# Lightning attention into a Mish layer: half of the second group's first layer by two sets of seven products, and buffers and sums placed anew

## The chip, the core and the metric

The kernel runs on one core of one Trainium2 chip. The metric is the device time of one execution, in microseconds (us), lower is better. The core has five engines with a queue of instructions each, which run in order and wait for each other on semaphores: TensorE (PE in the profile, its weight loads PEld), VectorE (DVE), ScalarE (ACT), GpSimd (POOL) and SyncE (SP).

## What is computed

The reference has two parts. The first is a decayed linear attention over 4 batches, 8 heads, 768 positions and head size 64, in blocks of positions with a running state:

```
intra = (q k^T * Dmask) v
inter = (q * lam_pow) kv_state
out   = intra + inter
kv_state = lam^block * kv_state + (k * rev_pow)^T v
```

The result, as 3072 tokens of 512 features, goes through two dense layers:

```
h = x @ w_in                      # 512 -> 2048
g = h * tanh(softplus(h))         # Mish
return g @ w_out                  # 2048 -> 512
```

Inputs and result are float32; the kernel computes products in float16 with float32 sums.

## The kernel before

**Groups and blocks.** The 768 positions are cut into six groups of 128 positions (n = 0 to 5); a group has four blocks, one for each batch (b = 0 to 3), and 512 tokens. The program is one order of steps written out by hand, in which attention of a later group is strewn between the dense products of an earlier one, so that TensorE always has a product to do while the other engines prepare the next operands.

**Attention of one block.** `turn_pe` (L222) transposes k and q on TensorE (L230) and copies the result out of PSUM, by ScalarE (L238) or VectorE (L236); `turn_dma` (L240) has the DMA engines do it for two blocks. `scores` (L251) makes the products of q and k in two PSUM banks, `be` and `bo`, and VectorE multiplies them by the mask (two `sb` tiles, L262). `outputs` (L279) sums state part (L283) and masked part (L288) in bank `bz`, and VectorE scales that into `xn` (L291). `state` (L336) multiplies the decayed k (`kd`, made by `decay_k`, L249) by v into bank `bH` (L332); VectorE adds the old state (`raw`, L344) and GpSimd multiplies by the decay (`w`, L346). `xn` is then transposed into `xt`, the first layer's input, by a DMA (L296) or on TensorE (L302, copied out at L307).

**First layer.** Two forms are in use. `two_units` (L381) makes two of the 16 slices of 128 features for half of the group's tokens (256) in eight products of 128x256, in one of the banks `bA`, `bB`, `bC` in turn, and ScalarE applies Mish (L391). The other form is a set of seven products (`set_of`, `set_step`, L425 and L452): a quarter of the features, for all 512 tokens, is seen as a 2x2 by 2x2 block product and made in seven block products of four matmuls each (L445) in place of eight, after the scheme of Strassen in Winograd's form. A set needs sums of weights (`wsum`, four per set by `w_sum`, L408), sums of the input (`xsum`, four per group by `x_sums`, L423), two copies by ScalarE (`seed` L459, `p5` L467), and two additions by VectorE: L470, which adds the copy to bank `o.b` and puts it in bank `o.c` before step m7 may write `o.b` again, and L474, which makes `c22` from `o.b` before step m4 may write it. The steps come in the order m1, seed, m2, m5, m6, m7, m3, m4. Before the change group 1 (the second) is made by `two_units` alone; groups 2 to 5 by sets.

**Second layer.** Group 0 goes plainly (`dense2_plain`, L604): per block four parts of four products of 128x512 in one bank, called as `plain2`. Later groups use seven products there as well (`dense2`, L566), from sums of the weights (`tsum`, `weight_sum`, L504) and of the Mish results (`gsum`, `token_sum`, L523, called as `sums`). The last group's second layer, `dense2_alone` (L618), closes the kernel: its last products are added in three pieces (L657) into output tiles of tag `osum`, of which there are three buffers, and stored by SP's queue (L531).

**Order around the change.** After group 1's attention the program runs the 16 calls of `two_units` for group 1 (each half of the tokens by itself), with attention of group 2's first two blocks, the weight sums of set 3 (`w_sum(3, ...)`) and of set 1, and the sums of w_out between them (L758 to L817); then `plain2` for group 0 with the attention of group 2's blocks 2 and 3 (L825 to L844); then the loop over n (L860).

Of the kernel before, what the change touches and what calls it, by code (L numbers as in the profile page):

```python
# [7 lines left out]
F32 = mybir.dt.float32  # L8
# [12 lines left out]
def kernel(  # L21
# [10 lines left out]
    nc = tc.nc  # L32
    B, H, S, D = q.shape
    C = 128
# [212 lines left out]
    def decay_k(n, b, eng):  # L247
        kd[n, b] = work.tile([128, H, D], F16, name="kd", tag="kd", bufs=4)
        eng.tensor_tensor(out=kd[n, b], in0=kn[n, b], in1=bc(lk, 2, D), op=ALU.mult)  # L249
# [131 lines left out]
    def two_units(n, ni, r):  # L381

        t = bank(next_bank(), [2, HC])
        cs = slice(r * HC, r * HC + HC)
        for u in range(2):
            for kc in range(NKC):
                m = (ni + u) % 4 * 128
                nc.tensor.matmul(  # L388
                    t[:, u, :], win[ni // 4][:, kc, m : m + 128], xt[n][:, kc, cs],
                    start=(u == 0 and kc == 0), stop=(kc == NKC - 1), skip_group_check=True)  # L390
        nc.scalar.activation(h_tile(n)[:, ni : ni + 2, cs], t, AF.Mish)  # L391
# [171 lines left out]
    def osum():  # L563
        return work.tile([128, 2, HN], F32, name="osum", tag="osum", bufs=3)
# [53 lines left out]
    def dense2_alone(n):  # L618

        x, z = bank("G", [2, HN]), bank("H", [2, HN])  # L620
        y = [(bank("A", [HN]), 0, 0, HN), (bank("B", [HN // 2]), 1, 0, HN // 2),
             (bank("C", [HN // 2]), 1, HN // 2, HN)]
        keep = lambda name: work.tile([128, 2, HN], F32, name=name, tag=name, bufs=1)

        def both(p, t, fresh):
            for blk in range(2):
                product(n, p, t[:, blk, :], blk, fresh and blk == 0)

        both(1, x, True)
# [12 lines left out]
        nc.gpsimd.tensor_tensor(out=u2, in0=u3, in1=p7, op=ALU.subtract)  # L642
        for t, blk, lo, hi in y:
            product(n, 5, t, blk, True, lo, hi)
        o = osum()
        for t, blk, lo, hi in y:
            nc.vector.tensor_tensor(out=o[:, blk, lo:hi], in0=t, in1=u3[:, blk, lo:hi], op=ALU.add)
        store(n, 1, 1, o)
        both(4, z, False)
        o = osum()  # L650
        nc.vector.tensor_tensor(out=o, in0=z, in1=p1, op=ALU.add)
        store(n, 1, 0, o)
        for t, blk, lo, hi in y:
            product(n, 3, t, blk, False, lo, hi)
        for t, blk, lo, hi in y:
            o = osum()
            nc.vector.tensor_tensor(out=o[:, blk, lo:hi], in0=t, in1=u2[:, blk, lo:hi], op=ALU.add)  # L657
            store(n, 0, 1, o[:, blk : blk + 1, lo:hi], blk, lo, hi)

# [110 lines left out]
    two_units(1, 6, 0)  # L770
    later[2]()
    out1(3, "G", "e", "o")
    two_units(1, 8, 0)
    later[3]()
    two_units(1, 10, 0)
    turn_pe(2, 0, ("H", "z"))
    decay_k(2, 0, nc.vector)
    decay_k(2, 1, nc.vector)
    w_sum(1, 0, nc.vector)
    w_sum(1, 1, nc.vector)  # L780
    two_units(1, 12, 0)
    turn_dma(2, 1)

    def attend(n, b):
        scores(n, b)

    def attended(n, b, turn=None):
        then = outputs(n, b, turn)
        state(n, b, "H", nc.gpsimd)
        return then  # L790

    two_units(1, 14, 0)
    attend(2, 0)
    two_units(1, 0, 1)
    w_sum(1, 2, nc.vector)
    w_sum(1, 3, nc.vector)
    turn_pe(2, 1, ("H", "G"))
    two_units(1, 2, 1)
    attended(2, 0)
    attend(2, 1)  # L800
    two_units(1, 4, 1)
    weight_sum(0, 0)
    two_units(1, 6, 1)
    weight_sum(0, 1)
    two_units(1, 8, 1)
    attended(2, 1)
    for t, bp in (("k", 0), ("q", 0), ("v", 0)):
        load_pair(t, 3, bp)
    for i in range(2):
        weight_sum(1, i)  # L810
    two_units(1, 10, 1)
    two_units(1, 12, 1)
    two_units(1, 14, 1)
    for i in range(4):
        w_sum(3, i, nc.vector)
    weight_sum(2, 0)
    weight_sum(2, 1)  # L817

    def plain2(b, *parts):
        for part in parts:
            dense2_plain(0, b, part, "GABC"[b])

    plain2(0, 0, 1, 2, 3)  # L825
    attend(2, 2)
    decay_k(2, 2, nc.vector)
    plain2(1, 0, 1)
    attended(2, 2)
    turn_dma(3, 0)  # L830
    attend(2, 3)
    decay_k(2, 3, nc.vector)
    plain2(1, 2, 3)
    plain2(2, 0)
    last_x = attended(2, 3, "e")
    for t, bp in (("k", 1), ("q", 1), ("v", 1)):
# [23 lines left out]
    for n in range(1, NG - 1):  # L860
# [110 lines left out]
            h(1)  # L971
        mm(0, "m5", "m6")
        if not fresh:
            sums(n, 1, 0, 1)
            h(1)
        o_(0)
        fetch(("k", 0), ("q", 0))
        if fresh:
            h(1)
# [11 lines left out]
        settle()  # L991
        mm(1, "m2")
        h(1)
        mm(1, "m5", "m6")
        sums(n, 1, 2)
        h(1)
        o_(1)
        fetch(("v", 0), ("k", 1))
# [69 lines left out]
```

## Time and profile before

| what | value |
|---|---|
| median of 3 runs | 201.73 us (201.51 to 202.71) |
| profiled execution, its own time | 201.52 us |
| its span, first to last instruction | 199.7 us |
| mean granted TensorE clock | 0.997 |
| TensorE busy | 192.3 us of 199.7 |
| VectorE busy | 154.3 us |
| ScalarE busy | 104.9 us |
| GpSimd busy | 80.7 us |

In the rows of the timeline stand start and duration in us, engine, line, operation, out<-in, shape of out and in, and the number of instructions merged; in brackets the idle time before them on that engine and what ended it. Instructions overlap by their pipelines, so the distance between two starts says what one costs in a full queue, and start plus duration says when its result is there. A row of the view of stretches has, for each engine, busy time and (xinstructions), then TensorE's granted clock and DMA figures.

### The profile page before, as it was taken

What the parts mean: (1) busy time and instruction counts of PE and PEld (TensorE: products, weight loads), DVE (VectorE), ACT (ScalarE), POOL (GpSimd) and SP (SyncE); (2) the same over time, 40 slices, a digit from 0 to 9 for tenths busy, and PEclk for the clock granted to TensorE, in tenths of its full rate; (3) what the DMA queues carried; (4) which work ended last, traced back from release to release, by engine and by line L of the source; (5) the groups of instructions that cost most, each with busy time, mean ns of one, the idle gap of its engine ahead of it and who ended that gap; (6) DMA issues with size and microseconds to landing.
All of it is one profiled execution on the core that took longest, in us unless ns stands there. A gap on an engine that the chain in (4) does not pass through costs nothing.

```text
span 199.7 us, 4828 instructions
## 1 busy us (share of the span) xinstructions
PE 192.3 (96%) x1991; PEld 155.0 (78%) x1991; DVE 154.3 (77%) x263; ACT 104.9 (53%) x194; POOL 80.7 (40%) x78
## 2 busy tenths in 40 slices
PE   7979999999999999999999999999999999999991
PEld 3757556898945569888988978988888988888891
DVE  6699879997999888799798698698588657179041
ACT  4885665567531233672467473468464574827300
POOL 7999465960482694499600674200000000000020
PEclk9999999999999999999999999999999999999998
DMA  8999999999999999999999499991112311003133
GB/s 131 137 152 202 173 181 156 165 206 204 159 142 174 199 167 159 177 118 168 182 200 188 50 85 162 170 219 53 29 28 80 82 53 53 3 2 108 53 105 105
DMA packets 107704, 25.87 MB, mean 130 GB/s; under 512 B 97826, under 2 KB 107170, under 8 KB 107682
## 3 DMA queue, kind: packets, MB, share of 16 engines
q0 software_dynamic: 77568, 13.37, 87.9%
q1 hardware_dynamic: 29072, 11.93, 31.0%
q10 hardware_dynamic: 1042, 0.26, 0.6%
q8 instruction: 15, 0.25, 0.5%
q14 instruction: 7, 0.06, 0.1%
HBM read 27.26 MB, written 6.29 MB: 168 GB/s over the span
## 4 chain that ended last, share of the span: by engine, by line
PE 81%; DMA 8%; POOL 7%; DVE 2%; issue 1%; ACT 0%; POOLq 0%; DVEq 0%
PE bG L560 15%; PE bH L560 13%; PE bB L445 8%; PE bC L445 7%; DMA win<-in_moe_w_in_dram 7%; PE bA L445 6%; PE be L256 3%; PE bC L388 3%; PE bA L388 2%; PE bB L388 2%; PE bz L283 2%; PE bz L288 2%; POOL win L96 2%; PE bA L611 2%; PE bB L611 2%; PE bC L611 2%
## 5 line engine op out<-in xcount | busy, mean ns | idle before, releaser
L346 POOL TENSOR_TENSOR w<-raw,lbm 128x512 f16<-128x512 f32 x14 | 19.6, 1402 | 40.1 <-DVE raw L344 40.1
L560 PEld LDWEIGHTS <-gsum 128*128 128x128 f16 x336 | 31.3, 98 | 3.5
L642 POOL TENSOR_TENSOR c<-p,u 128x512 f32<-128x512 f32 x1 | 1.3, 1271 | 63.7 <-DVE p L641 63.7
L445 PEld LDWEIGHTS <-wsum 128*128 128x128 f16 x256 | 24.7, 98 | 2.8
L560 PEld LDWEIGHTS <-hsg 128*128 128x128 f16 x240 | 22.9, 98 | 3.0
L445 PEld LDWEIGHTS <-win 128*128 128x128 f16 x192 | 18.4, 98 | 2.6 <-issue 0.3
L560 PE MATMUL bH<-tsum,gsum 128*128 128x256 f16 x160 | 20.4, 273 | 0.0
L560 PE MATMUL bG<-wout,hsg 128*128 128x256 f16 x160 | 19.8, 273 | 0.0
L262 DVE TENSOR_TENSOR sb<-be,dm 128x512 f16<-128x512 f32 x22 | 15.1, 686 | 3.3 <-PE bo L256 2.4
L445 PE MATMUL bA<-xt,win 128*128 128x256 f16 x112 | 16.8, 273 | 0.0
L449 ACT ACTIVATE hsg<-bC 128x512 f16<-128x512 f32 x14 | 8.3, 592 | 14.2 <-PE bC L445 14.1
L523 DVE TENSOR_TENSOR gsum<-hsg 128x1024 f16<-128x1024 f16 x20 | 15.6, 785 | 0.1
L262 DVE TENSOR_TENSOR sb<-bo,dm 128x512 f16<-128x512 f32 x22 | 15.0, 680 | 0.0
L291 DVE TENSOR_TENSOR xn<-bz,lq 128x512 f16<-128x512 f32 x18 | 12.3, 683 | 1.8 <-PE bz L288 1.2
L445 PE MATMUL bB<-xsum,wsum 128*128 128x256 f16 x88 | 13.2, 273 | 0.0
L388 PEld LDWEIGHTS <-win 128*128 128x128 f16 x128 | 12.0, 98 | 1.5
L87 POOL DMA_DIRECT2D kn<-in_k_dram x10 | 12.0, 1197 | 1.5 <-PE bB L362 1.5
L449 ACT ACTIVATE hsg<-bB 128x512 f16<-128x512 f32 x14 | 8.3, 596 | 7.8 <-PE bB L445 7.3
L87 POOL DMA_DIRECT2D vn<-in_v_dram x10 | 11.7, 1173 | 1.4 <-DMA win<-in_moe_w_in_dram 1.1
L87 POOL DMA_DIRECT2D qn<-in_q_dram x10 | 11.8, 1180 | 0.7 <-PE bA L362 0.7
L445 PE MATMUL bC<-xsum,wsum 128*128 128x256 f16 x80 | 12.0, 273 | 0.0
L470 DVE TENSOR_TENSOR bC<-bB,p 128x512 f32<-128x512 f32 x8 | 5.6, 700 | 7.5 <-PE bB L445 5.2
(192 smaller groups left out, 445.9 us busy)
## 6 DMA issues: line engine op xcount, KB each, us to landing
out_dram<-osum SPq DMA_DIRECT2D x23, 256.0 KB, 2.4
kn<-in_k_dram POOLq DMA_DIRECT2D x10, 256.0 KB, 9.3
qn<-in_q_dram POOLq DMA_DIRECT2D x10, 256.0 KB, 10.4
vn<-in_v_dram POOLq DMA_DIRECT2D x10, 256.0 KB, 10.0
wout<-in_moe_w_out_dram POOLq DMA_DIRECT2D x4, 512.0 KB, 15.1
win<-in_moe_w_in_dram POOLq DMA_DIRECT2D x3, 512.0 KB, 10.4
vz<-in_v_dram POOLq DMA_DIRECT2D x2, 256.0 KB, 6.0
kn<-in_k_dram POOLq DMA_DIRECT2D x3, 128.0 KB, 4.5
```

The costliest lines, as they stand in the source:

```text
L87: nc.gpsimd.dma_start(out=tile_, in_=rows(src, n, 2 * bp, 2))
L256: nc.tensor.matmul(p_[t][:, j, :], kT[n, b][rs, j, :], qT[n, b][rs, j, :], start=True, stop=True)
L262: nc.vector.tensor_tensor(out=sb[n, b, t], in0=p_[t], in1=dm[:, t], op=ALU.mult)
L291: nc.vector.tensor_tensor(out=xn, in0=po, in1=bc(lq, 2, D), op=ALU.mult)
L346: eng.tensor_tensor(out=w_new, in0=raw, in1=lbm, op=ALU.mult)
L388: nc.tensor.matmul(t[:, u, :], win[ni // 4][:, kc, m : m + 128], xt[n][:, kc, cs], start=(u == 0 and kc == 0), stop=(kc == NKC - 1), skip_ ...
L445: nc.tensor.matmul(t[:, u, :], lhs, rhs, start=(fresh and u == 0 and kk == 0), stop=(kk == 1), skip_group_check=True)
L449: nc.scalar.activation(h_tile(o.n)[:, 4 * o.s + 2 * r : 4 * o.s + 2 * r + 2, t * HC : t * HC + HC], src, AF.Mish)
L470: nc.vector.tensor_tensor(out=o.c, in0=o.b, in1=o.p5, op=ALU.add)
L523: nc.vector.tensor_tensor(out=gsum[n, i][:, ks, :], in0=a, in1=b, op=op)
L560: nc.tensor.matmul(t, lhs(kk, blk), rhs(kk)[:, lo:hi], start=(fresh and kk == 0), stop=(kk == HK - 1), skip_group_check=True)
L611: nc.tensor.matmul(po, hsg[n][:, ki, b * C : (b + 1) * C], wout[part][:, kk, :], start=(ki == 0), stop=(ki == NKI - 1))
```

## The change

Group 1's feature quarters 2 and 3 (units 8 to 15) are now made by two sets of seven products (`upper[0]`, `upper[1]`), units 0 to 7 still by `two_units`. What this brings with it: `x_sums(1, ...)` for group 1; `w_sum(3, ...)` earlier and `w_sum(1, ...)` later; group 2's k and q of block 0 and 1 transposed earlier and next to each other, with the copies of q by VectorE instead of ScalarE; `decay_k` of blocks 2 and 3 of group 2 on GpSimd instead of VectorE; `plain2` and `weight_sum` spread between the steps of the sets. In the loop some `sums` are moved by a step. In `dense2_alone` the first two of the last three output pieces get buffers of the tag `raw` (two), the third one of `osum`.

```diff
-            o = osum()
+            o = work.tile([128, 2, HN], F32, name="last", tag="osum" if lo else "raw", bufs=3 if lo else 2)
...
     out1(3, "G", "e", "o")
-    two_units(1, 8, 0)
+    turn_pe(2, 0, ("H", "z"), "k")
+    turn_pe(2, 0, (None, "z"), "q", True)
     later[3]()
-    two_units(1, 10, 0)
-    turn_pe(2, 0, ("H", "z"))
-    decay_k(2, 0, nc.vector)
-    decay_k(2, 1, nc.vector)
-    w_sum(1, 0, nc.vector)
-    w_sum(1, 1, nc.vector)
-    two_units(1, 12, 0)
+    turned_in = next_bank() + next_bank()
+    turn_pe(2, 1, turned_in, "k")
+    turn_pe(2, 1, turned_in, "q", True)
+    two_units(1, 0, 1)
     turn_dma(2, 1)
...
+    attend(2, 0)
+    two_units(1, 2, 1)
+    x_sums(1, 0, 1, 2, 3)
+    decay_k(2, 0, nc.vector)
+    two_units(1, 4, 1)
+    outputs(2, 0)
+    two_units(1, 6, 1)
+    state(2, 0, "H", nc.gpsimd)
+    attend(2, 1)
+    decay_k(2, 1, nc.vector)
+    upper = [set_of(1, 2, ("A", "B", "C")), set_of(1, 3, ("A", "C", "B"))]
...
+    mm1(0, "m1", "seed")
+    w_sum(3, 0, nc.vector)
+    w_sum(3, 1, nc.vector)
+    plain2(0, 0)
+    mm1(0, "m2", "m5")
+    attended(2, 1)
+    decay_k(2, 2, nc.gpsimd)
+    decay_k(2, 3, nc.gpsimd)
+    for t, bp in (("k", 0), ("q", 0), ("v", 0)):
+        load_pair(t, 3, bp)
+    mm1(0, "m6")
+    w_sum(3, 2, nc.vector)
+    w_sum(3, 3, nc.vector)
+    plain2(0, 1)
+    mm1(0, "m7", "m3")
+    weight_sum(0, 0)
+    weight_sum(0, 1)
+    mm1(1, "m1", "seed")
+    mm1(0, "m4")
+    plain2(0, 2)
+    mm1(1, "m2", "m5")
+    plain2(0, 3)
+    mm1(1, "m6")
+    weight_sum(1, 0)
+    plain2(1, 0)
+    mm1(1, "m7", "m3")
+    weight_sum(1, 1)
+    plain2(1, 1)
+    mm1(1, "m4")
     attend(2, 2)
-    decay_k(2, 2, nc.vector)
-    plain2(1, 0, 1)
+    for i in range(4):
+        w_sum(1, i, nc.vector)
+    weight_sum(2, 0)
+    plain2(1, 2)
     attended(2, 2)
     turn_dma(3, 0)
     attend(2, 3)
-    decay_k(2, 3, nc.vector)
-    plain2(1, 2, 3)
+    weight_sum(2, 1)
+    plain2(1, 3)
     plain2(2, 0)
...
         if not fresh:
-            sums(n, 1, 0, 1)
+            sums(n, 1, 0)
             h(1)
         o_(0)
+        if not fresh:
+            sums(n, 1, 1)
...
+        sums(n, 1, 2)
         mm(1, "m5", "m6")
-        sums(n, 1, 2)
         h(1)
```

How the queues move, at the three places of which the prediction speaks. The first is VectorE's queue just after group 1's attention (the rows ahead of it, to `raw<-bo`, are the same in both programs); a minus is a row of before, a plus one of the change.

```order
 L344 TENSOR_TENSOR raw<-bo,w_448 128x512
-L249 TENSOR_TENSOR kd<-kn,lk 128x512 x2
+L236 COPY qT<-bz 128x512
+L236 COPY qT<-bB 128x512
+L262 TENSOR_TENSOR sb<-be,dm 128x512
+L262 TENSOR_TENSOR sb<-bo,dm 128x512
+L423 TENSOR_TENSOR xsum_886<-xt 128x512
+L423 TENSOR_TENSOR xsum_888<-xt,xsum_886 128x512
+L423 TENSOR_TENSOR xsum_890<-xt 128x512
+L423 TENSOR_TENSOR xsum_892<-xt,xsum_888 128x512
+L249 TENSOR_TENSOR kd<-kn,lk 128x512
```

The two decayed k tiles stood first; now the copies of q, the first block's mask and the four sums of the input stand ahead of the first of them.

The second place is VectorE's queue from the second block's `kd` on: where the first set's additions L470 and L474 stand in the change.

```order
L249 TENSOR_TENSOR kd<-kn,lk 128x512
L408 TENSOR_TENSOR wsum_157<-win_74 128x512
L408 TENSOR_TENSOR wsum_157<-wsum_157,win_74 128x512
L291 TENSOR_TENSOR xn<-bz,lq 128x512
L344 TENSOR_TENSOR raw<-bH,w_422 128x512
L470 TENSOR_TENSOR bC<-bB,p_981 128x512
L408 TENSOR_TENSOR wsum_157<-win_74 128x512
L408 TENSOR_TENSOR wsum_157<-win_74,wsum_157 128x512
L474 TENSOR_TENSOR c_1032<-bB,p_981 128x512
```

At that time GpSimd has, behind the state of group 2's second block, two instructions that were VectorE's:

```order
 L346 TENSOR_TENSOR w_415<-raw,lbm 128x512
 L346 TENSOR_TENSOR w_422<-raw,lbm 128x512
+L249 TENSOR_TENSOR kd<-kn,lk 128x512 x2
 L87 DMA kn<-in_k_dram 128x16x64
 L87 DMA qn<-in_q_dram 128x16x64
```

So the third and fourth sum of weights stand between the two additions of the set, and GpSimd's new instructions come ahead of the loads of group 3.

The third place is VectorE's queue for blocks 2 and 3 of group 2. Before:

```order
L262 TENSOR_TENSOR sb<-be,dm 128x512
L262 TENSOR_TENSOR sb<-bo,dm 128x512
L249 TENSOR_TENSOR kd<-kn,lk 128x512
L291 TENSOR_TENSOR xn<-bz,lq 128x512
L344 TENSOR_TENSOR raw<-bH,w_441 128x512
L262 TENSOR_TENSOR sb<-be,dm 128x512
L262 TENSOR_TENSOR sb<-bo,dm 128x512
L249 TENSOR_TENSOR kd<-kn,lk 128x512
```

And with the change:

```order
L262 TENSOR_TENSOR sb<-be,dm 128x512
L262 TENSOR_TENSOR sb<-bo,dm 128x512
L408 TENSOR_TENSOR wsum_155<-win_72 128x512
L408 TENSOR_TENSOR wsum_155<-wsum_155,win_72 128x512
L408 TENSOR_TENSOR wsum_155<-win_72 128x512
L408 TENSOR_TENSOR wsum_155<-win_72,wsum_155 128x512
L504 TENSOR_TENSOR tsum_160<-wout_77,wout_75 128x1024
L291 TENSOR_TENSOR xn<-bz,lq 128x512
L344 TENSOR_TENSOR raw<-bH,w_441 128x512
L262 TENSOR_TENSOR sb<-be,dm 128x512
L262 TENSOR_TENSOR sb<-bo,dm 128x512
```

Five sums of weights took the place of one `kd` between block 2's mask and its `xn`.

More of the change, by code (lines that the diff above doesn't have):

```diff
@@ L790, in attended @@
         return then
[L792 to L817, printed above, removed]
     def plain2(b, *parts):
@@ L823, in plain2, with mm1 @@
             dense2_plain(0, b, part, "GABC"[b])
-    plain2(0, 0, 1, 2, 3)
+    attend(2, 0)
[9 more added lines that the diff above has]
+    upper = [set_of(1, 2, ("A", "B", "C")), set_of(1, 3, ("A", "C", "B"))]
+    def mm1(i, *steps):
+        for step in steps:
+            set_step(upper[i], step)
+    mm1(0, "m1", "seed")
[27 more added lines that the diff above has]
+    mm1(1, "m4")
     attend(2, 2)
-    decay_k(2, 2, nc.vector)
-    plain2(1, 0, 1)
+    for i in range(4):
+        w_sum(1, i, nc.vector)
+    weight_sum(2, 0)
+    plain2(1, 2)
     attended(2, 2)
```

## The prediction

> **What bounds the kernel now.** I began with the page: busy times and the chain that ended last, then stretches, then the timelines of single engines.
>
> ```profile
> PE 192.3 (96%) x1991; PEld 155.0 (78%) x1991; DVE 154.3 (77%) x263; ACT 104.9 (53%) x194; POOL 80.7 (40%) x78
> PE 81%; DMA 8%; POOL 7%; DVE 2%; issue 1%; ACT 0%; POOLq 0%; DVEq 0%
> 44.00:56.00 12.00, 12.00 (x143) 10.32 (x141) 10.96 (x17) 7.85 (x15) 3.86 (x4) 1.00 1.76 179
> 56.00:72.00 16.00, 16.00 (x117) 8.07 (x115) 14.53 (x22) 2.67 (x6) 9.63 (x9) 1.00 1.53 179
> 72.00:92.00 20.00, 20.00 (x225) 17.37 (x224) 16.82 (x27) 10.54 (x20) 14.48 (x12) 1.00 1.88 151
> ```
>
> TensorE bounds the kernel, at the full granted clock (1.00), and in the stretch that the change rewrites (41 to 72 us) it has no idle time at all. The fourth number of a stretch (after its length, PE and PEld) is VectorE: 10.96 of 12 and 14.53 of 16 us, 91% in both (16.82 of 20, 84%, in the loop behind it). TensorE's work is the first limit there; VectorE is a close second, with 2.5 us to spare in 28. What the change saves on TensorE must therefore be set against what it asks of VectorE, and above all when.
>
> ```profile
> 41.39 0.39 PE L332 MATMUL bo<-vn,kd 128*128 128x128 f16 x4
> 41.61 1.04 PE L388 MATMUL bA<-xt,win 128*128 128x256 f16 x8
> 42.49 0.39 PE L302 MATMUL bG<-ident,xn 128*128 128x128 f16 x4
> 42.71 1.04 PE L388 MATMUL bB<-xt,win 128*128 128x256 f16 x8
> 43.58 0.39 PE L230 MATMUL bH<-ident,kn 128*128 128x128 f16 x4
> ```
>
> Start to start, eight products of 128x256 cost 0.87 us (42.71 to 43.58), 0.109 us each; four of 128x128 cost 0.22; results come some 0.17 us after that. Four of 128x512 take as long as eight of 128x256.
>
> **What it removes on TensorE.** Group 1's first layer was 16 calls of eight products, 128; it becomes 8 calls and two sets of 7 x 4, 120. Eight fewer at 0.109: **-0.9 us**. All else on TensorE is only moved.
>
> **The head, a wait that fillers hid.** The calls of `two_units` between the last transposes are gone. After `bo<-vn,kd` (issued by 41.61) the transposes of k go to bank `bH`, which VectorE still reads:
>
> ```profile
> 41.04 0.68 DVE L344 TENSOR_TENSOR raw<-bH,w 128x512 f32<-128x512 f32 x1
> 41.64 0.68 DVE L291 TENSOR_TENSOR xn<-be,lq 128x512 f16<-128x512 f32 x1
> 43.18 0.59 ACT L307 ACTIVATE xt<-bG 128x512 f16<-128x512 f16 x1
> ```
>
> They start at 41.04+0.68+0.05, 41.77, 0.16 late. The `xn` of block 3 is there at 42.32, so its transposes start at 42.4 in place of 42.2. The next call, `two_units(1, 0, 1)`, needs block 3's `xt`: transposes issued by 42.62, results 0.17 later, a copy of 0.59, so 43.4, while TensorE has finished the other transposes at 43.06: 0.35 to 0.4 late. Together **+0.7** (0.4 to 0.9).
>
> **First VectorE chain, to step m7 of set 0.** Prices:
>
> ```profile
> 50.27 0.68 DVE L262 TENSOR_TENSOR sb<-be,dm 128x512 f16<-128x512 f32 x1
> 50.87 0.68 DVE L262 TENSOR_TENSOR sb<-bo,dm 128x512 f16<-128x512 f32 x1
> 47.51 0.42 DVE L408 TENSOR_TENSOR wsum<-win 128x512 f16<-128x512 f16 x1
> 47.84 0.42 DVE L408 TENSOR_TENSOR wsum<-win,wsum 128x512 f16<-128x512 f16 x1
> 57.74 0.69 DVE L504 TENSOR_TENSOR tsum<-wout,wout 128x1024 f16<-128x1024 f16 x1
> 60.63 0.68 DVE L249 TENSOR_TENSOR kd<-kn,lk 128x512 f16<-128x512 f16 x1
> 75.84 0.41 DVE L423 TENSOR_TENSOR xsum<-xt 128x512 f16<-128x512 f16 x1
> 76.97 0.42 DVE L423 TENSOR_TENSOR xsum<-xt,xsum 128x512 f16<-128x512 f16 x1
> ```
>
> In a full queue an operation on PSUM costs 0.60 (50.27 to 50.87), one on 512 float16 columns 0.33, four `xsum` 1.45 (75.84 to 76.97, and 0.33), `kd` and `tsum` 0.60 by their equal length. From block 0's mask to L470, VectorE's queue now holds two `sb` 1.2, four `xsum` 1.45, `kd` 0.6, `xn` and `raw` 1.2, two `sb` 1.2, `kd` 0.6, two `wsum` 0.8 (the second waits for the first), `xn` and `raw` 1.2, and L470 0.7: 8.95 us, nearly 9.2 with one meeting with GpSimd's `w` (below). It can begin 0.2 us after the first block's `scores` have been issued. TensorE, from the end of those `scores` to m7: three calls of `two_units` 2.6, two `outputs` 1.0, two `state` 0.45, one `scores` 0.33, m1, m2, m5, m6 at 0.44 each 1.75, two parts of `plain2` 1.75: 7.9 us. VectorE is 9.2+0.2-7.9 = 1.5 late. Part of it (0.45) falls earlier: `state(2, 0)` needs its `kd`, which now stands behind `xsum`, ready 0.2+1.2+1.45+0.7 = 3.55 after the `scores`, TensorE there after 3.1. In all **+1.4** (1.0 to 1.7).
>
> **Second chain, `c22` before m4.** Between L470 and L474 stand the third and fourth `wsum`, and at that moment GpSimd works too:
>
> ```profile
> 41.80 2.95 POOL L346 TENSOR_TENSOR w<-raw,lbm 128x512 f16<-128x512 f32 x2 [1.39 <-DVE raw L344]
> 42.83 2.47 DVE L249 TENSOR_TENSOR kd<-kn,lk 128x512 f16<-128x512 f16 x2
> 54.17 1.65 POOL L346 TENSOR_TENSOR w<-raw,lbm 128x512 f16<-128x512 f32 x1 [2.46 <-DVE raw L344]
> 54.00 2.36 DVE L504 TENSOR_TENSOR tsum<-wout,tsum 128x1024 f16<-128x1024 f16 x2
> ```
>
> Two `kd` should take 1.28 and took 2.47; they end at 45.30, 0.55 after GpSimd's second `w` (44.75). Two `tsum` should take 1.29 and took 2.36, ending at 56.36, 0.54 after `w` (55.82), which itself took 1.65 in place of 1.27. So VectorE's sums out of SBUF and GpSimd's operations stand still for each other, and after one of VectorE's GpSimd gets its turn. Now `w` of block 1 starts when `raw` is done, one operation (0.6) before the third `wsum`, which so waits for some 0.8; behind `w` stand the two `kd` that were given to GpSimd (1.03 to 1.5 each); the first takes its turn ahead of the fourth `wsum`. The two `wsum` take about 2.4 in place of 0.67. L474's result so comes 0.6+2.4+0.7 = 3.7 after the start of L470, and m7 starts 0.7 after that same start; from there TensorE has m7, m3 and set 1's m1, 1.3 us, and then waits: 3.7-0.7-1.3, **+1.7** (0.1 if neither blocks, 0.9 if only `w` does, 1.9). I take the upper end, as both rows above show the turn being given.
> The Trainium skill, SBUF — State Buffer, section "Who interferes with whom", has a VectorE instruction with two SBUF inputs and a GpSimd instruction that reads SBUF block each other, the first to issue holding the port for its whole length. The rows above agree (1.2 and 1.1 us of blocking); by issue order alone the fourth `wsum` could also come first, and the wait would be the 0.9 of the range.
>
> **Third chain, blocks 2 and 3.** Set 1's additions leave VectorE time again. But from block 2's `scores` on, VectorE has two `sb` 1.2, four `wsum` 1.45, `tsum` 0.6, `xn`, `raw` 1.2, two `sb` 1.2 to a result at 5.75, begun 0.5 after the start of the `scores`: 6.2. TensorE needs the last `sb` in block 3's `outputs`, and has until there two `scores` 0.66, three parts of `plain2` 2.6, `outputs` 0.5, `state` 0.22 and four products 0.22: 4.2 us. **+2.0** (1.5 to 2.3), 0.4 of it at block 2's own `outputs`, where one part of `plain2` (0.87) now covers two masks. Nothing is behind that which could give it back: TensorE is the bound from there to the end, so stalls and savings add up.
>
> **Later stretch.** The one stall of the loop that VectorE makes:
>
> ```profile
> 113.09 0.70 DVE L470 TENSOR_TENSOR bB<-bC,p 128x512 f32<-128x512 f32 x1 [1.77 <-ACT p L467]
> 113.70 1.53 DVE L523 TENSOR_TENSOR gsum<-hsg 128x1024 f16<-128x1024 f16 x1
> 116.48 0.60 PE L445 MATMUL bC<-xsum,win 128*128 128x256 f16 x4 [0.21 <-DVE c L474]
> ```
>
> The moved `sums` put that `gsum` ahead of L470, into the 1.77 us in which VectorE stood idle. This takes away the 0.2 and about as much lost just before: **-0.4** (-0.5 to 0).
>
> **The tail.**
>
> ```profile
> 195.02 0.61 PE L560 MATMUL bC<-wout,gsum 128*128 128x128 f16 x8
> 195.27 0.28 DVE L657 TENSOR_TENSOR osum<-bB,c 128x128 f32<-128x128 f32 x1
> 196.91 0.29 DVE L657 TENSOR_TENSOR osum<-bC,c 128x128 f32<-128x128 f32 x1 [1.35 <-DMA out_dram<-osum]
> ```
>
> The last piece waits 1.35 us for a store to free its buffer. With two pieces in `raw` buffers, the third takes the oldest `osum`, long stored, and starts when its bank is ready, 195.63+0.05: 1.2 us sooner. The last store follows it; it may queue a little behind two others. **-1.2** (-1.3 to -0.8).
>
> **Sum.** -0.9 +0.7 +1.4 +1.7 +2.0 -0.4 -1.2 = +3.3. The profiled execution took 201.52 us (span 199.7, 1.8 around it) and lies 0.2 under the median of 201.73. 201.5+3.3 = **204.8 us**.
> What I cost at nothing: the q copies moved to VectorE (0.34 each) stand in an idle time, since they end before block 0's `scores`; ScalarE's seeds and copies of the sets, 0.5 each, are covered by a part of `plain2` each; the `tsum` that move back behind the sets are read only by group 1's second layer, after 72 us; group 3's loads, issued some 2 us later behind the `kd` on GpSimd, have time (rival three).
>
> **The rivals.**
> *One: VectorE keeps up (other side).* If the sets run as in the loop, where TensorE was busy in 20.00 of 20 us, the three chains and the head's waits go and only the savings stand: -0.9-0.4-1.2 = -2.5, 199.0 us. It decides from the point at which the first chain is under 7.9 us. For it: the same additions are hidden in the loop. Against it: the loop loads VectorE with 84% there, this place stood at 91% before, and the rows' distances leave no room for 9 us in 7.9. Chance 0.06.
> *Two: the blocking hardly bites.* GpSimd's `w` starts late, or VectorE's two `wsum` go through first: the second chain is 0.1 to 0.9 in place of 1.7, and the other two come out at their low ends (1.0, 1.5): 204.8-1.2-0.9 = 202.7. For it: the meeting depends on a few tenths of a us. Against: `w` is released by the `raw` just ahead. Chance 0.19.
> *Three: a transposed load comes late as well.*
>
> ```profile
> 55.76 1.20 POOL L87 DMA_DIRECT2D kn<-in_k_dram  x1
> 65.31 2.88 SPq L243 DMA_TRANSPOSE qT<-qn  x1
> 74.21 0.23 PE L256 MATMUL be<-qT,kT 64*128 64x128 f16 x1
> ```
>
> Group 3's loads are now behind two `kd`, and its transposes behind block 2's `xn`, which is later. Between the last transpose's issue (65.31) and its use (74.21) lie 8.9 us, and a transpose of this kind lands in a median 7.1 on the page. I see no stall, as its use moves too; 2 us more than expected would make it 206.8. Chance 0.06.
>
> ```profile
> qT<-qn SPq DMA_TRANSPOSE x7, 7.1
> ```
>
> **How the numbers follow.** My forecast has the remaining 0.69. The range holds 8 in 10: 202.5, just below rival two, to 206.2, where the chains are at their upper ends (+0.2, +0.3, +0.2, +0.3 over the sum, with nothing gained at 116 us). A difference of 1%, 2 us, is about what a measurement of this kernel can tell from no change, so slower means over 203.7: the forecast and rival three but for their lower edge, 0.75; within 1%: rival two and that edge, 0.19; faster: rival one, 0.06.
>
> **What would show it.** In the changed profile TensorE has idle time between 41 and 72 us, released by VectorE: near 0.5 at `bH<-vn,kd` of block 0, 1 at m7 of set 0 (`bB<-xsum,wsum`, waiting for L470), 1.8 at its m4 (`bB<-xsum,win`, waiting for L474), 2 at block 3's `bz<-vn,sb`. Two `wsum` that should take 0.7 take over 2. At the end the wait of L657 for a store is gone. If TensorE shows no idle time there, or its idle time has other releasers, the prediction is wrong; if the second chain alone is short, rival two was right.

## The result and the profile after

| | before | after |
|---|---|---|
| median | 202.18 us (201.51 to 202.71, 4 runs) | 205.07 us (204.92 to 205.26, 4 runs) |
| ratio to before, 95% interval | | 1.0133 [1.0092, 1.0173] |
| profiled execution | 201.52 us | 204.99 us |
| span | 199.7 us | 203.2 us |

The changed kernel is slower by some 1.3%. Forecast were 204.8 us, in a range of 202.5 to 206.2. Here and below, medians and ratios leave out any execution that took over 1.5% more than the fastest of its kernel: four of the kernels below had one each. The page of the changed kernel, the lines that answer to those of before:

```profile
PE 192.9 (95%) x1983; PEld 154.0 (76%) x1983; DVE 155.6 (77%) x271; ACT 106.2 (52%) x196; POOL 82.5 (41%) x80
PE 75%; DVE 8%; POOL 7%; DMA 7%; issue 1%; ACT 1%; POOLq 0%; DVEq 0%; ACTq 0%
```

TensorE has eight products fewer (1991 to 1983), and VectorE eight operations more. On the chain that ended last VectorE's share went from 2% to 8%. A sum of busy times would have told little of this: VectorE is at 77% as before. (TensorE's busy time even rose, by 0.6 us. A row's duration reaches 0.17 us past the start of the next row in a full queue, 0.60 against 0.435, so each of the ten stalls below would add about that much busy time: by this estimate 1.7 less the 0.9 that was saved.) The stretches show where it sits:

```profile
41.00:56.00 15.00, 13.32 (x155) 10.15 (x153) 13.75 (x25) 7.53 (x14) 6.26 (x6) 1.00 1.65 184
56.00:72.00 16.00, 13.74 (x112) 8.07 (x112) 12.75 (x23) 5.59 (x10) 6.04 (x6) 1.00 1.13 127
78.00:98.00 20.00, 20.00 (x225) 17.37 (x224) 16.71 (x28) 10.42 (x19) 14.52 (x13) 1.00 1.67 153
```

Where TensorE (the second number) had no idle time before, it now misses 1.7 of 15 and 2.3 of 16 us; in the loop behind it, it is full again at 20.00 of 20. The clock is 1.00 throughout. The timeline of TensorE names the places:

```profile
43.54 1.03 PE L388 MATMUL bC<-xt,win 128*128 128x256 f16 x8 [0.24 <-ACT xt L307]
48.34 0.40 PE L332 MATMUL bH<-vn,kd 128*128 128x128 f16 x4 [0.26 <-DVE kd L249]
54.09 0.60 PE L445 MATMUL bB<-xsum,wsum 128*128 128x256 f16 x4 [0.74 <-DVE bC L470]
56.90 0.60 PE L445 MATMUL bB<-xsum,win 128*128 128x256 f16 x4 [1.33 <-DVE c L474]
65.43 0.38 PE L288 MATMUL bz<-vn,sb 128*128 128x64 f16 x7 [0.16 <-DVE sb L262]
69.29 0.20 PE L288 MATMUL bz<-vn,sb 128*128 128x64 f16 x1 [0.82 <-DVE sb L262]
69.89 0.38 PE L288 MATMUL bz<-vn,sb 128*128 128x64 f16 x7 [0.40 <-DVE sb L262]
```

The number in brackets counts from the modelled end of the product before. What a stall costs is how far the distance of two starts exceeds the usual one (0.435 for four products of 128x256); by that these seven cost 0.40, 0.43, 0.90, 1.50, 0.32, 0.98 and 0.57 us. Three of 0.16 stand without a bracket, two in the head and one at m7 of the second set (61.39). Together 5.6 us, mostly released by VectorE.

**Two rows that measure the stage.** Executions start a little apart, so I measure between two instructions that all the kernels share: the first product of the outputs of block 2 of group 1 (L283, near 39 us), and a call of L560 just behind a `scores`, at 75 to 81 us, where the loop is already running. (The call has eight products; its rows here are cut by the end of the window shown, and only their start is used.) Of before, then of after:

```profile
39.09 0.40 PE L283 MATMUL bz<-w,qT 128*128 128x128 f16 x4
74.54 0.72 PE L560 MATMUL bG<-wout,hsg 128*128 128x256 f16 x5
```

```profile
39.17 0.40 PE L283 MATMUL bz<-w,qT 128*128 128x128 f16 x4
79.42 0.83 PE L560 MATMUL bG<-wout,hsg 128*128 128x256 f16 x6
199.40 0.61 PE L560 MATMUL bC<-wout,gsum 128*128 128x128 f16 x8
```

That is 35.45 before and 40.25 after: the rewritten stage costs 4.80 us. From there to the last product it is 195.02-74.54 = 120.48 before and 199.40-79.42 = 119.98 after: the moved sums give back 0.50. From the last product to the end of the span it is 4.68 before and 3.80 after: the new buffers of the tail give back 0.88. With 0.08 of a later start this makes 4.80-0.50-0.88+0.08 = 3.50, the difference of the spans.

These are single executions. The one of before, 201.52 us, is at the low end of its four, so the medians lie only 2.9 us apart, and the interval of the ratio allows 1.9 to 3.5. The stage itself repeats well: the two other traces below whose program leaves it as it was and whose transposes came in time (runs 1 and 9) have 35.45 again.

### The profile page after: what moved, and what is told of

Read it like the earlier page. It is cut to its first block, busy times and chain, and to the rows that moved or that the text cites. A ratio compares the mean times of both kernels' runs of the same rounds, so it can differ in the third digit from the quotient of the medians.

```text
span 203.2 us, 4832 instructions
## 1 busy us (share of the span) xinstructions
PE 192.9 (95%) x1983; PEld 154.0 (76%) x1983; DVE 155.6 (77%) x271; ACT 106.2 (52%) x196; POOL 82.5 (41%) x80
## 4 chain that ended last, share of the span: by engine, by line
PE 75%; DVE 8%; POOL 7%; DMA 7%; issue 1%; ACT 1%; POOLq 0%; DVEq 0%; ACTq 0%
PE bG L560 16%; PE bH L560 13%; PE bB L445 9%; PE bC L445 8%; DMA win<-in_moe_w_in_dram 7%; PE bA L445 6%; PE be L256 3%; DVE sb L262 2%; PE bz L288 2%; POOL win L96 2%; PE bC L611 2%; PE bz L283 2%; POOL kn L82 1%; PE bC L388 1%; DVE wsum L408 1%; POOL qn L82 1%
## 5 line engine op out<-in xcount | busy, mean ns | idle before, releaser
L560 PEld LDWEIGHTS <-gsum 128*128 128x128 f16 x336 | 31.3, 98 | 3.5
L445 PEld LDWEIGHTS <-wsum 128*128 128x128 f16 x288 | 27.8, 98 | 4.8 <-issue 1.3
L560 PEld LDWEIGHTS <-hsg 128*128 128x128 f16 x240 | 22.9, 98 | 3.0
L445 PEld LDWEIGHTS <-win 128*128 128x128 f16 x216 | 20.7, 98 | 4.7 <-issue 1.5
L560 PE MATMUL bH<-tsum,gsum 128*128 128x256 f16 x160 | 20.4, 273 | 0.0
L560 PE MATMUL bG<-wout,hsg 128*128 128x256 f16 x160 | 19.8, 273 | 0.0
L445 PE MATMUL bA<-xt,win 128*128 128x256 f16 x128 | 19.2, 273 | 0.0
L449 ACT ACTIVATE hsg<-bC 128x512 f16<-128x512 f32 x16 | 9.5, 592 | 17.4 <-PE bC L445 17.4
L445 PE MATMUL bB<-xsum,wsum 128*128 128x256 f16 x100 | 15.0, 272 | 0.7 <-DVE bC L470 0.7
L449 ACT ACTIVATE hsg<-bB 128x512 f16<-128x512 f32 x16 | 9.5, 596 | 9.5 <-PE bB L445 9.0
L523 DVE TENSOR_TENSOR gsum<-hsg 128x1024 f16<-128x1024 f16 x20 | 14.4, 724 | 0.1
L445 PE MATMUL bC<-xsum,wsum 128*128 128x256 f16 x92 | 13.8, 273 | 0.0
L449 ACT ACTIVATE hsg<-bA 128x512 f16<-128x512 f32 x16 | 9.6, 597 | 6.9 <-PE bA L445 6.9
L470 DVE TENSOR_TENSOR bB<-bC,p 128x512 f32<-128x512 f32 x7 | 4.9, 700 | 9.6 <-PE bC L445 6.0
```

What stands on the lines that cost most here:

```text
L445: nc.tensor.matmul(t[:, u, :], lhs, rhs, start=(fresh and u == 0 and kk == 0), stop=(kk == 1), skip_group_check=True)
L449: nc.scalar.activation(h_tile(o.n)[:, 4 * o.s + 2 * r : 4 * o.s + 2 * r + 2, t * HC : t * HC + HC], src, AF.Mish)
L470: nc.vector.tensor_tensor(out=o.c, in0=o.b, in1=o.p5, op=ALU.add)
L523: nc.vector.tensor_tensor(out=gsum[n, i][:, ks, :], in0=a, in1=b, op=op)
L560: nc.tensor.matmul(t, lhs(kk, blk), rhs(kk)[:, lo:hi], start=(fresh and kk == 0), stop=(kk == HK - 1), skip_group_check=True)
```

## The experiments

The theory is that of the prediction: TensorE's stalls come from VectorE, whose operations on this stage stand in an order in which the ones that TensorE waits for are behind others that nobody waits for yet; GpSimd's operations prolong some of them. One rival says that the sets of seven themselves cost more than they save here, whatever the order; another that the stalls go elsewhere when one is removed, because VectorE is simply full.

All ratios are to the kernel before, timed beside it on the same chip; medians of different runs come from different chips. "Stage" is the distance between the two rows above.

| kernel | median us (runs) | ratio, 95% interval | stage us | from there to the last product |
|---|---|---|---|---|
| after | 205.07 (4) | 1.0133 [1.0092, 1.0173] | 40.25 | 119.98 |
| tail alone | 201.19 (9) | 0.9959 [0.9925, 0.9993] | 35.45 | 120.49 |
| moved sums alone | 202.13 (10) | 0.9996 [0.9961, 1.0032] | 37.13 | 119.98 |
| tail and moved sums | 200.77 (7) | 0.9934 [0.9908, 0.9960] | 35.45 | 119.98 |
| sums behind c22 | 203.93 (8) | 1.0086 [1.0056, 1.0116] | 39.07 | 119.97 |
| sums out of blocks 2 and 3 | 203.63 (9) | 1.0074 [1.0040, 1.0108] | 38.75 | 120.02 |
| kd behind the loads | 204.21 (4) | 1.0106 [1.0070, 1.0142] | 39.40 | 119.97 |
| kd first | 205.22 (4) | 1.0163 [1.0118, 1.0209] | 40.18 | 119.98 |
| kd of blocks 0 and 1 on GpSimd | 204.73 (4) | 1.0127 [1.0078, 1.0177] | 39.52 | 120.03 |
| chains cleared | 201.26 (11) | 0.9961 [0.9937, 0.9986] | 36.43 | 119.98 |

**1. The tail alone.** Before, with only the new output buffers:

```diff
-            o = osum()
+            o = work.tile([128, 2, HN], F32, name="last", tag="osum" if lo else "raw", bufs=3 if lo else 2)
```

> The kernel before with one edit of the change: the first two of the last three output pieces in raw buffers. Theory (the edits' prices add up, the tail's is the wait of 1.35 us for a store): 1.2 us under the kernel before, the last L657 starting some 0.1 us after its bank is ready. Rival (the stores queue behind each other, so that an earlier last piece lands no earlier): within 0.4 us of before.

The end of its timeline, TensorE's last product and VectorE's last addition:

```profile
195.30 0.61 PE L560 MATMUL bC<-wout,gsum 128*128 128x128 f16 x8
196.01 0.29 DVE L657 TENSOR_TENSOR last<-bC,c 128x128 f32<-128x128 f32 x1 [0.21 <-PE bC L560]
```

The last addition follows the last product by 0.71 us in place of 1.89, and waits for the product, no longer for a store: 1.18 sooner. But the span from the last product on became only 0.88 shorter (195.30 to 199.1 against 195.02 to 199.7), and the ratio makes it 0.8 (its interval allows 0.1 to 1.5): less than the theory's 1.2, more than the rival's 0.4. So 0.3 of it goes to the store behind: from the end of the last addition to the end of the span it takes 2.8 us, where it took 2.5. Stage and loop are as before.

**2. The moved sums alone.** Before, with the two steps of `sums` moved in the loop:

```diff
-            sums(n, 1, 0, 1)
+            sums(n, 1, 0)
             h(1)
         o_(0)
+        if not fresh:
+            sums(n, 1, 1)
...
+        sums(n, 1, 2)
         mm(1, "m5", "m6")
-        sums(n, 1, 2)
```

> The kernel before with only the moved sums of the loop. Theory: the gsum of 113.7 us goes into VectorE's idle time ahead of L470, and the two short stalls of TensorE at 115.9 and 116.5 us (0.1 and 0.27 over the usual distance) go: 0.4 us faster. Rival (the stall only moves on to the next addition, since the sum in between costs the same 0.6 us): no change within 0.2 us.

Its times show no gain. Its trace shows the expected 0.5 in the loop (119.98 against 120.48), and a loss of 1.68 in the stage, in which nothing was changed:

```profile
63.56 0.69 DVE L291 TENSOR_TENSOR xn<-bz,lq 128x512 f16<-128x512 f32 x1 [2.34 <-DMA xt<-xn]
```

VectorE waited 2.34 us for a transposing DMA that was still reading the buffer; these transposes landed in a median of 8.0 us between 55 and 70 us, against 6.6 in before. Whether that lateness belongs to this kernel or to this one execution can't be told from here; by itself the run is inconclusive. The ninth run, which has the same edit, took the question up again: its stage is 35.45, so the loss isn't there in every execution of it.

**3. The third and fourth sum of weights behind c22.** After, with

```diff
     mm1(0, "m6")
-    w_sum(3, 2, nc.vector)
-    w_sum(3, 3, nc.vector)
     plain2(0, 1)
     mm1(0, "m7", "m3")
+    w_sum(3, 2, nc.vector)
+    w_sum(3, 3, nc.vector)
```

> The changed kernel with the third and fourth weight sum of set 3 behind L474 instead of ahead of it. Theory VectorE (its queue and its blocking with GpSimd delay c22): the idle time ahead of m4 of set 0 (1.50 us) falls under 0.2, and 1.2 to 1.5 us of the whole time go, up to 0.3 of it given back at m5 of set 1, which waits for the weight sums. Theory sets (a set's own hand-over from bank to bank takes that long wherever VectorE's other work stands): the idle time stays within 0.3 us of 1.50.

The stage is 1.18 shorter than that of after; the medians are 1.1 apart, the ratios 0.95 us, with intervals that overlap, as they do in runs 4, 5 and 7. TensorE's m7, set 1's m1 and m4, and VectorE's rows for it:

```profile
54.64 0.60 PE L445 MATMUL bB<-xsum,wsum 128*128 128x256 f16 x4 [0.75 <-DVE bC L470]
55.51 0.60 PE L445 MATMUL bA<-xt,win 128*128 128x256 f16 x4
56.09 0.60 PE L445 MATMUL bB<-xsum,win 128*128 128x256 f16 x4
```

```profile
55.35 0.69 DVE L474 TENSOR_TENSOR c<-bB,p 128x512 f32<-128x512 f32 x1 [0.76 <-POOL w L346]
55.95 0.66 DVE L408 TENSOR_TENSOR wsum<-win 128x512 f16<-128x512 f16 x1
56.54 1.26 DVE L408 TENSOR_TENSOR wsum<-win,wsum 128x512 f16<-128x512 f16 x1
```

With L474 ahead of the two sums, m4 starts 0.58 after m1, 0.14 more than the usual distance, where it had lost 1.50. (The bracket of L474 names GpSimd's `w`, which ended at 55.33. But L474 also needs m7, which ended at 55.24; so `w` can account for 0.1 at most.) The sums are still slow (0.66 and 1.26), but only 0.17 of that is paid, at m5 of the second set. The stall before m7 (0.90) is where it was, since nothing ahead of it changed.

**4. Sums of weights out of blocks 2 and 3.** After, with the four `w_sum` of set 1 in VectorE's idle time before the second set's first addition, and both `weight_sum(2)` in the loop:

```diff
     mm1(1, "m2", "m5")
+    for i in range(4):
+        w_sum(1, i, nc.vector)
...
     attend(2, 2)
-    for i in range(4):
-        w_sum(1, i, nc.vector)
-    weight_sum(2, 0)
     plain2(1, 2)
...
-    weight_sum(2, 1)
...
-            weight_sum(3, 0)
+            weight_sum(2, 0)
+            weight_sum(2, 1)
...
+            weight_sum(3, 0)
```

(The first place in the code is just ahead of `plain2(0, 3)`; the last ones are in the loop.)

> The changed kernel with the four weight sums of set 1 moved into VectorE's idle time ahead of set 1's first addition (58 to 60.6 us), and the two sums of w_out that stood at blocks 2 and 3 moved into the loop. Theory VectorE: the idle time of TensorE at block 3's outputs (0.98 and 0.57) falls to 0.2 or less, block 2's 0.32 stays, and the whole time falls by 1.3 to 1.8 us. Rival, given back later: the sums that are moved into the loop stall it there, as VectorE is 84% busy in it, and less than 0.7 us of the whole time goes.

TensorE at block 2's outputs and at block 3's:

```profile
65.52 0.38 PE L288 MATMUL bz<-vn,sb 128*128 128x64 f16 x7 [0.16 <-DVE sb L262]
68.34 0.51 PE L288 MATMUL bz<-vn,sb 128*128 128x64 f16 x8
```

Block 3's products now run as eight without a break: its 0.98 and 0.57 are gone and come back nowhere. The stage is 1.50 shorter, the loop the same although it holds two sums more. Block 2's own 0.32 stays, as nothing in VectorE's queue stands there but the two masks.

**5. GpSimd's kd behind the loads.** After, with

```diff
     attended(2, 1)
-    decay_k(2, 2, nc.gpsimd)
-    decay_k(2, 3, nc.gpsimd)
     for t, bp in (("k", 0), ("q", 0), ("v", 0)):
         load_pair(t, 3, bp)
+    decay_k(2, 2, nc.gpsimd)
+    decay_k(2, 3, nc.gpsimd)
```

> The changed kernel with GpSimd's two kd behind its three loads of group 3 instead of ahead of them; VectorE's queue is untouched. Theory blocking (the fourth weight sum waits for the turn of GpSimd's kd): the fourth weight sum falls from 1.26 us to under 0.5, the idle time ahead of m4 from 1.50 to 0.6 to 0.8, and 0.6 to 0.9 us of the whole time go. Rival queue length (VectorE is late by the sheer number of operations): no change within 0.2 us; and if the loads of group 3 mattered, issued some 2 us earlier, TensorE would have less idle time after 72 us, where it has none.

This run takes the blocking apart. In the changed kernel, VectorE from behind L470 to L474, and GpSimd beside it:

```profile
53.95 1.11 DVE L408 TENSOR_TENSOR wsum<-win 128x512 f16<-128x512 f16 x1
54.98 1.26 DVE L408 TENSOR_TENSOR wsum<-win,wsum 128x512 f16<-128x512 f16 x1
56.16 0.68 DVE L474 TENSOR_TENSOR c<-bB,p 128x512 f32<-128x512 f32 x1
```

```profile
53.51 1.27 POOL L346 TENSOR_TENSOR w<-raw,lbm 128x512 f16<-128x512 f32 x1 [2.62 <-DVE raw L344]
54.74 2.41 POOL L249 TENSOR_TENSOR kd<-kn,lk 128x512 f16<-128x512 f16 x2
```

In the kernel of this run, where the issue of the loads stands behind `w` on GpSimd and the `kd` come later:

```profile
53.86 1.11 DVE L408 TENSOR_TENSOR wsum<-win 128x512 f16<-128x512 f16 x1
54.89 0.41 DVE L408 TENSOR_TENSOR wsum<-win,wsum 128x512 f16<-128x512 f16 x1
```

The third sum takes 1.11 in both, beside the same `w`. The fourth takes 0.41 in place of 1.26: the 0.85 were the first `kd`, which got its turn between VectorE's two sums. The stage is 0.85 shorter, of which m4's stall accounts for all (1.50 to 0.65). Of the 1.50, then, 0.85 came from the `kd`; the rest, 0.65, is `w` and the two sums themselves. (The prediction had 0.9 for `w` alone.)

**6. Block 0's kd ahead of the sums of the input.** After, with

```diff
-    x_sums(1, 0, 1, 2, 3)
     decay_k(2, 0, nc.vector)
+    x_sums(1, 0, 1, 2, 3)
```

> The changed kernel with block 0's kd ahead of the four sums of the input. Theory chain (VectorE has 9 us of work ahead of the first addition of set 0, whatever its order, and TensorE 7.9): the 0.43 us ahead of state of block 0 goes and comes back in full at the next wait, and the whole time stays within 0.2 us. Rival (each wait is local, the kd simply stands too far back): 0.4 us faster.

```profile
49.29 0.39 PE L332 MATMUL bH<-vn,kd 128*128 128x128 f16 x4
52.81 0.40 PE L332 MATMUL bH<-vn,kd 128*128 128x128 f16 x4
55.41 0.60 PE L445 MATMUL bB<-xsum,wsum 128*128 128x256 f16 x4 [0.90 <-DVE bC L470]
```

The stall at the first block's state is gone (no bracket at 49.29), but 0.22 appears at the second block's (52.81) and m7's grows from 0.90 to 1.06: 1.28 in place of 1.33, and a stage shorter by 0.07, which is nothing. (The 1.4 us by which its rows are later than those of after stood at the start already.) A stall that is taken out of a chain that is late as a whole moves to the chain's end. Only here did a stall move so: in runs 3 to 5, 0.17 us at most came back elsewhere.

**7. The same chain, made shorter.** After, with the `kd` of blocks 0 and 1 taken off VectorE:

```diff
     two_units(1, 0, 1)
+    decay_k(2, 0, nc.gpsimd)
+    decay_k(2, 1, nc.gpsimd)
...
-    decay_k(2, 0, nc.vector)
...
-    decay_k(2, 1, nc.vector)
```

> The changed kernel with the kd of blocks 0 and 1 of group 2 on GpSimd, which has been idle from 44.4 to 49.6 us, instead of VectorE: 1.4 us less in VectorE's first chain. Theory chain: the waits of 0.43 and 0.90 fall together by 0.7 to 0.9 us (not by all 1.33, since xn, raw and L470 follow block 1's outputs with only 1.5 us of products for 2.1 us of operations), and the whole time by as much. Rival blocking: GpSimd's operations hold up the sums of the input as long as they last, and less than 0.3 us is won.

```profile
53.62 0.60 PE L445 MATMUL bB<-xsum,wsum 128*128 128x256 f16 x4 [0.46 <-DVE bC L470]
```

The stall at the first state is gone, m7's went from 0.90 to 0.62, and the stage is 0.73 shorter. The times agree in direction alone: 0.3 us less, well within their intervals. Two operations of 0.6 taken from the chain gave 0.7, not 1.2. Most of the rest is another wait, which VectorE has now and had not in after:

```profile
51.67 0.69 DVE L291 TENSOR_TENSOR xn<-bz,lq 128x512 f16<-128x512 f32 x1 [0.23 <-PE bz L288]
```

L470 stands behind the second block's `xn` and `raw`, and these wait for that block's outputs on TensorE, which come behind m5. From the second sum of weights to `xn` it is 0.66 us in place of 0.34; another 0.1 each goes to the first `xsum` and the first of those sums of weights, which now run beside GpSimd's `kd` and `w` (0.53 and 0.52 in place of 0.42 and 0.41). A shorter queue alone brings L470 no earlier than that `xn` and `raw` allow. The next run has m6 ahead of those outputs for this reason; with it L470, which follows m6, comes ahead of that `xn` and `raw` in VectorE's queue too.

**8. All the chains cleared.** After, with edits 3, 5 and 7, and with more: set 1's four `w_sum` on GpSimd, both `weight_sum(2)` in the loop, and m6 of the first set ahead of `attended(2, 1)`:

```diff
+    mm1(0, "m6")
     attended(2, 1)
-    decay_k(2, 2, nc.gpsimd)
-    decay_k(2, 3, nc.gpsimd)
     for t, bp in (("k", 0), ("q", 0), ("v", 0)):
         load_pair(t, 3, bp)
-    mm1(0, "m6")
-    w_sum(3, 2, nc.vector)
-    w_sum(3, 3, nc.vector)
+    decay_k(2, 2, nc.gpsimd)
+    decay_k(2, 3, nc.gpsimd)
+    for i in range(4):
+        w_sum(1, i, nc.gpsimd)
     plain2(0, 1)
     mm1(0, "m7", "m3")
+    w_sum(3, 2, nc.vector)
+    w_sum(3, 3, nc.vector)
```

> The changed kernel with VectorE's first stretch of group 2 unloaded at every place where TensorE stood still: the gradients kd of blocks 0 and 1 are made on GpSimd right after the gates of group 1, those of blocks 2 and 3 on GpSimd behind the block's three loads, the four sums of W_in parts for set 1 on GpSimd behind them, the last two sums for set 0 on VectorE behind the addition that opens m4, the sums of W_out for sets 2 and 3 in the later loop, and m6 of set 0 is computed ahead of the outputs of block 1. Nothing is left out of the computation. If the two sets of seven save their eight matmuls (0.9 us) and the loss is only VectorE's queue, then m7 of set 0, m4 and block 3's outputs wait at most 0.2 us each, 0.7 stays in the head and 0.4 at block 2's outputs; by the sum of the stalls in the trace of the change that is 3.5 to 4.7 us less than the change, 200.4 to 201.6, and a ratio to before of 0.992 to 0.999. If the sets themselves cost (the stage stays bound by VectorE, or GpSimd becomes late with w or kd in its place), a stall of over 1 us in sum comes back between 45 and 72 us and the time is 202 or more, a ratio over 1.000.

(The "gradients kd" of this text are the decayed k tiles, and the "gates of group 1" GpSimd's `w`.)

```profile
39.11 0.40 PE L283 MATMUL bz<-w,qT 128*128 128x128 f16 x4
52.69 0.60 PE L445 MATMUL bB<-xsum,wsum 128*128 128x256 f16 x4
54.14 0.60 PE L445 MATMUL bB<-xsum,win 128*128 128x256 f16 x4
59.01 0.60 PE L445 MATMUL bC<-xsum,wsum 128*128 128x256 f16 x4 [0.21 <-DVE bB L470]
63.05 0.38 PE L288 MATMUL bz<-vn,sb 128*128 128x64 f16 x7 [0.16 <-DVE sb L262]
65.88 0.51 PE L288 MATMUL bz<-vn,sb 128*128 128x64 f16 x8
75.54 1.05 PE L560 MATMUL bG<-wout,hsg 128*128 128x256 f16 x8
```

```profile
51.60 0.70 DVE L470 TENSOR_TENSOR bC<-bB,p 128x512 f32<-128x512 f32 x1 [0.47 <-ACT p L467]
52.20 0.68 DVE L291 TENSOR_TENSOR xn<-bz,lq 128x512 f16<-128x512 f32 x1
```

L470 now stands ahead of `xn` and waits for ScalarE's copy alone. The first set's m7 (52.69) and block 3's outputs (65.88) no longer wait, m4 (54.14) loses 0.14. The stage falls from 40.25 to 36.43, and the median to 201.26, as the theory had it (200.4 to 201.6). What is left between 45 and 72 us, 1.0 us in sum, stands just at the mark where the rival was to count; a new stall at GpSimd's `w` or `kd` isn't among it. Of the 5.6 us of stalls 1.7 are left: 0.72 in the head, untouched; 0.14 at m4, 0.17 at m5 and 0.37 at m7 of the second set; 0.32 at block 2's outputs.

**9. Tail and moved sums, without the sets.** Before, with edits 1 and 2 together.

> The kernel before with the two parts of the change that have nothing to do with the sets of seven: the last results go to a buffer of their own, and one sum of the pair is moved behind the loop's additions. The theory that both pay as my prediction summed them expects 1.6 us less than before (a ratio of 0.992). The rival, that the moved sums pay nothing and only the tail does, expects 0.8 to 1.2 us less (0.994 to 0.996). Beside the kernel with the chains cleared it also says what the sets are worth: if that one is not under this one, the sets of seven pay nothing in this place even without the waits.

```profile
40.34 0.40 PE L283 MATMUL bz<-w,qT 128*128 128x128 f16 x4
75.79 0.94 PE L560 MATMUL bG<-wout,hsg 128*128 128x256 f16 x7
195.77 0.61 PE L560 MATMUL bC<-wout,gsum 128*128 128x128 f16 x8
```

Ratio 0.9934: 1.3 us less than before, between the theory's 1.6 and the rival's 0.8 to 1.2, and with an interval (0.8 to 1.9) that allows both. The trace has a stage as before (35.45), 0.50 from the moved sums and 0.85 from the tail. This kernel has the lowest ratio of the study, though its interval overlaps those of runs 1 and 8. The stage of the eighth is 0.98 longer than its stage, and its median 0.5 higher: 0.9 us saved, some 1.8 lost. That the order, and the split of work between VectorE and GpSimd, was at fault is shown for 3.8 of 4.8 us; that the sets pay in this place is not. What the best of my orders left over is still more than they save.

## Why the prediction was right

By its own steps, in us; the measured numbers are distances of starts in the traces of after and, for the loop and the tail, of the kernels that have the edit alone:

| term | forecast | measured |
|---|---|---|
| eight products fewer | -0.9 | -0.8 (what is left of the stage's 4.8 without its stalls of 5.6) |
| head | +0.7 (0.4 to 0.9) | 0.16+0.16+0.40 = 0.72 |
| first chain | +1.4 (1.0 to 1.7) | 0.43+0.90 = 1.33 |
| c22 before m4 | +1.7 (0.1 to 1.9) | 1.50 |
| blocks 2 and 3 | +2.0 (1.5 to 2.3) | 0.32+0.98+0.57 = 1.87 |
| not forecast: m7 of the second set | 0 | 0.16 |
| moved sums in the loop | -0.4 (-0.5 to 0) | -0.50 |
| tail | -1.2 (-1.3 to -0.8) | -0.88 |
| sum | +3.3 | +3.4 (3.5 with the later start of 0.08) |

The mechanism was right for the head, the three chains, the loop and the tail: the places, what is waited for there, and the order of size. The eight products were not measured by themselves. The wait that was not forecast, at m7 of the second set, is for its L470, which ended at 61.34, just ahead of m7. That the sums agree to 0.2 us is in part luck. The three chains were forecast 0.4 too long together, and that is made up for by the tail, which gave 0.3 less than forecast, and by the wait that was not forecast. And the measured sum is that of two single executions; the medians differ by 2.9.

**The head** came at both its places and for the reasons named: bank `bH`, `xn`, and `xt` copied by ScalarE. I found no work to put under it, and no run tried it; that the sets, which need the inputs of all four blocks, can't fill this place as calls of `two_units` on two blocks did, is argued only.

**The first chain** is a chain as said. Undoing one place of it moved the stall (run 6); taking work out of it shortened it (run 7). The prediction counted it as nothing but VectorE's queue, and for the changed kernel that holds: from block 0's mask on VectorE has no idle time there. The wait that run 7 laid bare, under a queue 1.2 us shorter, was not in the prediction; the expectation of that run had it.

**The second chain** was the term with the widest bounds, and its upper end, which the prediction leaned on, was right: run 5 shows the fourth sum at 1.26 us with `kd` waiting and 0.41 without, and run 3 shows that the order of L474 alone decides whether anybody pays for it. The two sums took 1.11 and 1.26 us, 2.21 from the start of the first to the start of L474, where 2.4 was forecast; that is the 0.2 by which the term is too large. The Trainium skill, SBUF — State Buffer, section "Who interferes with whom", calls the pair of ports that VectorE shares with GpSimd an exclusive lock, and says of VectorE's two-port modes that whoever issues first has it for the whole instruction. The traces agree on the length (the third sum ends 0.28 us after GpSimd's `w`). They add the turn: GpSimd's next operation, which waits, goes ahead of VectorE's next. Rival two, the 202.7, rested on the other order, and fell.

**The third chain** was sized within 0.13, and run 4 shows its cause: with the sums of weights gone from the queue at the two blocks, block 3's 1.55 goes entirely. That it fits "nothing behind gives it back" is seen in the loop, 119.98 long in nearly all these kernels, whatever the stage before it took.

**Moved sums.** 119.97 to 120.03 against 120.48, in every trace with the edit and in none without. The timeline of after shows the mechanism:

```profile
116.00 0.68 DVE L523 TENSOR_TENSOR gsum<-hsg 128x1024 f16<-128x1024 f16 x1
117.94 0.70 DVE L470 TENSOR_TENSOR bB<-bC,p 128x512 f32<-128x512 f32 x1 [1.26 <-ACT p L467]
120.85 0.60 PE L445 MATMUL bC<-xsum,win 128*128 128x256 f16 x4
```

The `gsum` stands in the idle time ahead of L470, as forecast, and m4 (the last row) no longer waits for L474: it starts 0.23 after the row before it, where in before it was 0.60. By the times it is not shown alone (run 2); between runs 1 and 9 the ratio falls by 0.0025, 0.5 us, with intervals that overlap.

**The tail** is the term that was furthest off, by 0.3, though within its bounds. The forecast counted the addition's 1.2 and named the queue of stores behind it, but took nothing off for it in the sum; 0.3 go there. The last addition of after, and the issue of the last store in before and in after:

```profile
200.10 0.29 DVE L657 TENSOR_TENSOR last<-bC,c 128x128 f32<-128x128 f32 x1 [0.21 <-PE bC L560]
```

```profile
197.23 0.33 SPq L531 DMA_DIRECT2D out_dram<-osum  x1
```

```profile
200.60 0.40 SPq L531 DMA_DIRECT2D out_dram<-last  x1
```

The last addition ends at 200.39 and the span at 203.2, 2.8 us later; in before it was 2.5 (197.20 to 199.7). SP issues the last store 0.21 after the addition, where it was 0.03: the store before it was issued only at 200.11 and took 0.40. The rest, 0.1, is the time from issue to landing (1.7 us, in before 1.6).

Rival one (199.0, VectorE keeps up) is refuted by the stalls, and run 8 says more: even with the queue unloaded at each place but the head, 1.7 us of them stay. For rival three (a transposed load is late) there is no stall behind 72 us in the changed kernel.

## What to carry to other kernels

Price a saving on the bound engine together with the queue order of the engine that feeds it: start at the row that releases a chain, add up everything in the queue up to the row that the bound engine waits for, and compare that with the work that the bound engine has until there; a share of busy time (91% here) doesn't show it, and the sum over such chains did, each to 0.2 us. In an in-order queue, put what nobody waits for behind what somebody does: by the stage, moving two sums gave 1.2 us and moving six gave 1.5, with what they cost elsewhere taken off. And take a mixed change apart: the two small parts of this one that have nothing to do with its name are worth 1.3 us alone.

## What was not expected of the hardware

- A row of sums out of SBUF beside GpSimd's operations is not blocked once but at each operation that GpSimd has waiting: 1.11 us beside `w` and then 1.26 beside `kd`, where an unblocked one takes 0.41. How this adds up depends on how many operations stand on each side.
- Two `tsum` took 2.97 us in run 8, while GpSimd issued loads, and 1.52 in run 4, while GpSimd ended a `kd` and then issued loads as well. In run 8 the loads were issued from 54.78 to 58.28:

```profile
55.37 2.97 DVE L504 TENSOR_TENSOR tsum<-wout 128x1024 f16<-128x1024 f16 x2
```

  Here it made L470 late, and m7 of the second set lost 0.37 for it. In run 4 four `wsum` beside such loads took 0.41 to 0.42 each. What tells the cases apart stays open.
- The sums of weights cost GpSimd far more than VectorE: three of set 1's four took 1.15 us each in run 8, where VectorE takes 0.41.
